# A decay attention and two MLPs on one core: the second products' first two blocks side by side, and another order of the work

## The chip, the core and the metric

The kernel runs on one core of a Trainium2 chip. Five engines work side by side, each through its own instructions in order: TensorE (PE: matrix products into PSUM), VectorE (DVE), ScalarE (ACT), GpSimd (POOL) and SyncE (SP, which here only issues DMAs). The metric is the device time of one execution in microseconds; three runs of the kernel before gave 709.08 to 711.84, median 710.28.

## The reference

Three parts follow each other. The attention has batch 2, 8 heads, 768 positions, head size 64; per block of positions it is `(q k^T * decay) v + (q * decay) state`, and the state takes in `k^T v`. Its output, as 1536 tokens of 512 numbers, goes through two MLPs without residual:

```
h = x @ w_in            # 1536x512 @ 512x2048
x = (h * cos(h)) @ w_out        # first MLP (layer 0); the second has h * sigmoid(h) (layer 1)
```

All is float32.

## The kernel before

**Accuracy.** Matrix products of the MLPs run on a reduced float format. Each operand is split in a high part (a cast on ACT) and a low part (original minus high, on POOL), and a product takes three matmuls: high by high, low by high, high by low. `split` (L122) does it for weights (`win`, `wout`), activations (`gh`, `gl`) and inputs (`xah`/`xal`, `xbh`/`xbl`). Weights are loaded as `raw` (three staging buffers), and made float by an ACT pass (L106) and two DVE passes (L117, L118).

**Attention** (L701 to L738): six chunks of 128 positions. TensorE transposes k and q, makes scores `psc`, multiplies with the state and with v into `pso`; DVE scales the scores (`at`, L326) and keeps the state (L308); `att_x` (L351) takes `pso` out as the first MLP's input with differences `xt`.

**First products** (`gemm_in`, L481): a scheme with seven products instead of eight for a 2x2 division of the operands. A "quad" is a pair of 128-wide slices of the hidden layer, j = 0 to 7, for part A (1024 tokens, 512 columns a matmul) or part B (512 tokens, 256 columns). Each of its seven products takes six matmuls into the PSUM banks a, b (one tile `cab`) and d. Between them ACT copies bank a to b (`copy_ab`, L412) and b to `u2`, `u4` (L416), DVE adds them to d (L421, L424), and the function is applied: in layer 0 `act_n` (L433), `act_s` (L442, DVE), `act_sin` (L449) and `act_g` (L455, DVE), which writes `gd` to DRAM. Products of the next quad are issued between those of the current one.

**Second products** (`gemm_outs`, L652): three blocks of 512 tokens one after the other, four PSUM banks `y` each. Per hidden slice f (16) `prepare` loads `gf` for two slices (L534), splits one (ACT L124, POOL L127), and twelve matmuls follow (L573). During block 0 the weights f = 4 to 15 are converted as well. `keep_a0`, `keep_a1`, `keep_b` turn layer 0's `y` into layer 1's input; `send` writes layer 1's.

Nothing reorders the work: each engine's instructions stand in the order in which the code calls them (a manual schedule), with tasks hung on loop steps by tables in the main loop. Tiles come from pools with a given number of buffers, and an instruction waits until its buffer is free. All large loads and stores go through SP's queue in order: an issue that waits for a buffer holds up those behind it.

Of the kernel before, what the change touches and what calls it, by code (L numbers as in the profile page):

```python
# [16 lines left out]
P = 128  # L17
# [22 lines left out]
def tile_decay_attention__two_mlps(  # L40
# [70 lines left out]
    def convert_w(*piece):  # L111
        if piece not in w32:
            rebias_w(*piece)
# [8 lines left out]
    def split(engine, hi, lo, of):  # L122
        if engine is nc.scalar:
            nc.scalar.copy(hi, of)  # L124
        else:
            engine.tensor_copy(hi, of)
        nc.gpsimd.tensor_tensor(out=lo, in0=of, in1=hi.bitcast(F32), op=ALU.subtract)  # L127
# [14 lines left out]
    def split_plain(L, j):  # L142
        t = wring[j // 2 % 2].tile([P, 2, UNITS, 2 * P], F32R, name="win")
        win[L, j] = t
        w0, w1 = w32.pop((L, 2 * j, 0)), w32.pop((L, 2 * j + 1, 0))
        split(nc.scalar, t[:, 0, 0:2].rearrange("p u c -> p (u c)"), t[:, 1, 0:2].rearrange("p u c -> p (u c)"), w0)
        split(nc.scalar, t[:, 0, 2], t[:, 1, 2], w1[:, 2 * P:])

    def split_sums(L, j):
        t = win[L, j]  # L150
        s = sums.pop((L, j))
        for i in range(2):
            u = slice(3 + 2 * i, 5 + 2 * i)
            split(nc.scalar, t[:, 0, u], t[:, 1, u], s[:, 2 * i:2 * i + 2])

    def split_out(L, f):
        t = wring[0 if f < 7 else 1].tile([P, 2, TB], F32R, name="wout")
        split(nc.scalar, t[:, 0], t[:, 1], w32.pop((L, f, 1)))
        wout[L, f] = t

    def pair_tasks(L, j):
        f = 2 * j
        return [
            lambda: (convert_w(L, f, 0), load_next()),
            lambda: (convert_w(L, f + 1, 0), load_next()),
            lambda: (sum_w(L, j), split_plain(L, j)),
# [3 lines left out]
    def out_tasks(L, f):  # L170
        return [lambda: (convert_w(L, f, 1), load_next()), lambda: split_out(L, f)]
# [48 lines left out]
    qkv, tr, at, kd, sdec, state, pkv, po = {}, {}, {}, {}, {}, {}, {}, {}  # L220
# [130 lines left out]
    def att_x(c):  # L351
        part, n = ("A", c) if c < CA else ("B", c - CA)
        h, l = (x[:, :, :, n * P:(n + 1) * P] for x in x_tiles(0, part))
        ps = po.pop(c).rearrange("p b (u t) i -> p b u t i", t=2)
        b1, b2 = ps[:, 0], ps[:, 1]
        xc = ap_2.tile([P, B, 2, P], F32, tag="xc", name="xc", bufs=1)
        t = ap_2.tile([P, 4, 2, P], F32, tag="xt", name="xt", bufs=1)
        nc.scalar.copy(xc, ps[:, :, 0])
        nc.scalar.copy(h[:, 0:2], b1)
        nc.scalar.copy(h[:, 2], b2[:, 1])  # L360
        nc.vector.tensor_tensor(out=t[:, 0], in0=b2[:, 0], in1=xc[:, 0], op=ALU.subtract)
        nc.vector.tensor_tensor(out=t[:, 1], in0=b2[:, 1], in1=t[:, 0], op=ALU.subtract)
# [95 lines left out]
    def ends(Q):  # L458
        return [
            lambda: (act_sin(Q, 0), act_s(Q, 1)),  # L460
            lambda: act_g(Q, 0),
            lambda: act_sin(Q, 1),
            lambda: act_g(Q, 1),
        ]

    def gemm_in(L, tasks, begun):

        qs = quads[L]
        if not begun:
            product(qs[0], 1)  # L470
            product(qs[0], 7)
            copy_ab(qs[0])
            late = keep_b()
            late.pop(0)()
            product(qs[0], 6)
            late.pop(0)()
            product(qs[0], 2)
            tasks[0] = late + tasks[0]
        copy_u(qs[0], "u2")
        old = []  # L480
        for n, Q in enumerate(qs):  # L481
            more = list(tasks.get(n, []))

            def task():
                if more:
                    more.pop(0)()

            def end():
                if old:
                    old.pop(0)()  # L490

            nxt = qs[n + 1] if n + 1 < len(qs) else None
            if nxt:
                product(nxt, 1)
            end()
            if nxt:
                copy_ab(nxt)
            task()
            product(Q, 5)
            copy_u(Q, "u4")  # L500
            c22(Q)
            end()
            if nxt:
                product(nxt, 7)
                product(nxt, 6)
                copy_u(nxt, "u2")
            else:
                gemm_out(L, 0, 0, (0, 1))
            end()
            task()  # L510
# [3 lines left out]
            end()  # L514
            act_n(Q, 0)
            act_s(Q, 0)
            if not nxt:
                gemm_out(L, 0, 1, (0, 1))
                prepare(L, 0, 2)
# [3 lines left out]
            while more:  # L523
                task()
            old = ends(Q)
        for x in old:
            x()


    gf, gt, ys = {}, {}, {}  # L530

    def load_g(L, b, j):
        t = tpool.tile([P, 2, TB], F32, tag="t4", name="gf", bufs=4)
        nc.sync.dma_start(  # L534
            out=t, in_=gd[L][2 * j:2 * j + 2, :, b * TB:(b + 1) * TB].rearrange("f p c -> p f c")
        )
        gf[L, b, j] = t

    def prepare(L, b, f):
        if f >= FT:  # L540
            b, f = b + 1, f - FT
            if b == NB:
                return
        if (L, b, f // 2) not in gf:
            load_g(L, b, f // 2)
        t = gf[L, b, f // 2][:, f % 2]
        gh, gl = (tpool.tile([P, TB], F32R, tag="t2", name=n, bufs=5) for n in ("gh", "gl"))
        split(nc.scalar, gh, gl, t)
        gt[L, b, f] = gh, gl
# [11 lines left out]
    def gemm_out(L, b, f, ms=range(4)):  # L561
# [15 lines left out]
    def keep_a0():  # L577

        y = ys[0, 0]
        h, l = x_tiles(1, "A")  # L580
        kept["x0"] = yring.tile([P, 4, TB], F32, name="x0")

        def one(u):
            nc.scalar.copy(h[:, u], y[u])
            nc.scalar.copy(kept["x0"][:, 2 * u:2 * u + 2], y[u])
            nc.vector.tensor_tensor(out=l[:, u], in0=y[u], in1=h[:, u].bitcast(F32), op=ALU.subtract)

        return [lambda: one(0), lambda: one(1)]

    def keep_a1():  # L590
        y = ys[0, 1]
        h, l = x_tiles(1, "A")
        x0 = kept["x0"]
        b12 = yring.tile([P, 2, TB], F32, name="b12")
        t = [yring.tile([P, 2, TB], F32, name="T") for _ in range(4)]

        def first():
            nc.scalar.copy(b12, y[0])
            nc.vector.tensor_tensor(out=t[0], in0=y[0], in1=x0[:, 0:2], op=ALU.subtract)

        def second(i):
            nc.scalar.copy(h[:, 2, i], y[4 + i])
            nc.vector.tensor_tensor(out=t[1][:, i], in0=y[4 + i], in1=t[0][:, i], op=ALU.subtract)
            nc.vector.tensor_tensor(out=t[2][:, i], in0=y[4 + i], in1=b12[:, i], op=ALU.subtract)
            nc.vector.tensor_tensor(out=l[:, 2, i], in0=y[4 + i], in1=h[:, 2, i].bitcast(F32), op=ALU.subtract)

        def third(i):
            if i == 3:
                nc.vector.tensor_tensor(out=t[3], in0=x0[:, 2:4], in1=t[1], op=ALU.subtract)
            for m in range(2):  # L610
                split(nc.scalar, h[:, 3 + i, m], l[:, 3 + i, m], t[i][:, m])

        return [first, lambda: second(0), lambda: second(1)] + [lambda i=i: third(i) for i in range(4)]

    def keep_b():
# [7 lines left out]
        def sub(o, x, z):  # L623
            nc.vector.tensor_tensor(out=o, in0=x, in1=z, op=ALU.subtract)

        def first():
            nc.scalar.copy(yc, y[0])
            nc.scalar.copy(h[:, 0], b11)
            sub(t[0], b12, yc[:, :, 0:HB])
            sub(l[:, 0], b11, h[:, 0].bitcast(F32))  # L630

        def second():
            nc.scalar.copy(h[:, 1], b21)
            nc.scalar.copy(h[:, 2], b22)
            sub(t[1], b22, t[0])
# [5 lines left out]
        def third(i):  # L641
            split(nc.scalar, h[:, 3 + i], l[:, 3 + i], t[i])
# [3 lines left out]
    def send(b, m):  # L646
        o = tpool.tile([P, TB], F32, tag="u", name="o", bufs=3)
# [4 lines left out]
    def gemm_outs(L, tasks):  # L652

        for b in range(NB):
            for f in range(FT):
                if L == 1 and b == NB - 1 and f >= FT - 2:
                    break
                prepare(L, b, f + 2) if (b, f) != (0, 0) else None
                if b == 0 and f < 2:
                    gemm_out(L, b, f, (2, 3))  # L660
# [161 lines left out]
```

## Time and profile before

| | us |
|---|---|
| median of three runs | 710.28 (709.08 to 711.84) |
| the profiled execution: its own time, its span | 713.8, 712.0 |
| TensorE busy (matmul) | 601.7 (85%) |
| POOL, ACT, DVE busy | 348.1, 313.1, 286.6 |

TensorE's busy time holds stretches at half clock, so it is not the work at full speed. The stages, by the starts of instructions in the trace: attention to 62.0, hand-over to 91.8, first products of layer 0 to 238.2, second products to 412.5; layer 1 the same to about 552.8 and 708.2; then the last output. In the groups below, a row of the timeline gives the engine's idle time before the instruction in brackets, and what ended it.

### The profile page before, as it was taken

How to read it: one execution, taken by the hardware profiler on the slowest of the kernel's cores; microseconds unless marked ns; L12 is line 12 of the kernel's file. 1: busy time of each engine (PE TensorE's matmuls, PEld its weight loads, DVE VectorE, ACT ScalarE, POOL GpSimd, SP SyncE). 2: the span in 40 equal slices, each digit the busy share in tenths (PEclk: the TensorE clock that was granted, in tenths of full speed). 3: DMA queues.
4: the chain of work that ended last, by engine and by line, in shares of the span. 5: the costliest groups of instructions: out<-in, count | busy, mean ns of one | idle time of the engine just before them, and what ended most of it. 6: DMA issues, size and time to landing. Idle time of an engine off the chain costs nothing.

```text
span 712.0 us, 8935 instructions
## 1 busy us (share of the span) xinstructions
PE 601.7 (85%) x3313; PEld 484.6 (68%) x3313; DVE 286.6 (40%) x397; ACT 313.1 (44%) x518; POOL 348.1 (49%) x299
## 2 busy tenths in 40 slices
PE   8887588888887667889996897999998566999996
PEld 5776366777776545678884676877777444788884
DVE  5674336566664643310044025544455444300101
ACT  4444256677765533342253246555545234322220
POOL 3456435444422266545469816554433366644542
PEclk9998799999999899899999999999999899999999
DMA  9991125344434454643303303654435646352611
GB/s 181 217 226 61 60 59 178 118 149 149 147 133 164 156 177 168 200 130 113 90 5 119 112 1 118 196 176 162 148 137 184 211 174 207 102 166 59 200 38 59
DMA packets 83324, 97.06 MB, mean 136 GB/s; under 512 B 40784, under 2 KB 57168, under 8 KB 83280
## 3 DMA queue, kind: packets, MB, share of 16 engines
q1 hardware_dynamic: 81040, 95.96, 43.1%
q10 hardware_dynamic: 2240, 0.53, 0.4%
q8 instruction: 26, 0.43, 0.3%
q14 instruction: 18, 0.15, 0.1%
HBM read 68.16 MB, written 28.31 MB: 135 GB/s over the span
## 4 chain that ended last, share of the span: by engine, by line
PE 53%; ACT 14%; DMA 11%; DVE 9%; issue 5%; POOL 5%; SPq 2%; POOLq 0%; ACTq 0%; DVEq 0%
PE y L573 25%; PE cab L394 19%; DMA gf<-gd 10%; PE d L394 5%; ACT s L433 3%; ACT u L416 2%; ACT gh L124 2%; ACT w L106 2%; DVE w L118 2%; POOL gl L127 2%; ACT s L449 2%; DVE s L455 2%; PE pso L346 1%; DVE h L424 1%; DVE s L442 1%
## 5 line engine op out<-in xcount | busy, mean ns | idle before, releaser
L127 POOL TENSOR_TENSOR gl<-gf,gh 128x512 fp32r<-128x512 f32 x96 | 131.3, 1368 | 138.4 <-PE y L573 80.9
L124 ACT CAST gh<-gf 128x512 fp32r<-128x512 f32 x96 | 59.4, 619 | 176.7 <-PE y L573 108.9
L573 PE MATMUL y<-gh,wout 128*128 128x512 f32 x384 | 128.2, 417 | 0.0
L573 PE MATMUL y<-wout,gh 128*128 128x512 f32 x384 | 119.6, 393 | 0.0
L394 PE MATMUL cab<-xah,win 128*128 128x512 f32 x320 | 92.9, 413 | 21.0 <-ACT u L416 9.5
L573 PE MATMUL y<-gl,wout 128*128 128x512 f32 x192 | 82.6, 430 | 29.1 <-POOL gl L127 29.1
L118 DVE SCALAR_TENSOR_TENSOR w<-w,sb 128x512 uint32<-128x512 uint32 x64 | 55.2, 862 | 110.9 <-ACT w L106 106.9
L573 PE MATMUL y<-wout,gl 128*128 128x512 f32 x192 | 77.3, 403 | 21.4 <-POOL gl L127 19.5
L573 PEld LDWEIGHTS y<-gh,wout 128*128 128x128 f32 x384 | 78.8, 205 | 17.0
L394 PEld LDWEIGHTS cab<-xah,win 128*128 128x128 f32 x320 | 58.4, 195 | 40.1 <-ACT u L416 15.4
L573 PEld LDWEIGHTS y<-wout,gh 128*128 128x128 f32 x384 | 73.0, 190 | 14.9
L394 PE MATMUL cab<-xbh,win 128*128 128x256 f32 x320 | 56.1, 299 | 19.7 <-ACT u L416 13.5
L573 PEld LDWEIGHTS y<-gl,wout 128*128 128x128 f32 x192 | 39.1, 204 | 44.2 <-POOL gl L127 36.4
L127 POOL TENSOR_TENSOR wout<-w,wout 128x512 fp32r<-128x512 f32 x32 | 44.7, 1396 | 49.9 <-ACT wout L124 49.9
L394 PEld LDWEIGHTS cab<-xbh,win 128*128 128x128 f32 x320 | 46.8, 193 | 28.3 <-ACT u L416 17.6
L573 PEld LDWEIGHTS y<-wout,gl 128*128 128x128 f32 x192 | 36.5, 190 | 34.8 <-POOL gl L127 25.3
L139 POOL TENSOR_TENSOR S<-w 128x256 f32<-128x256 f32 x32 | 27.8, 869 | 60.9 <-DVE w L118 60.9
L394 PE MATMUL cab<-xal,win 128*128 128x512 f32 x160 | 51.0, 400 | 0.0
L127 POOL TENSOR_TENSOR win<-S,win 128x512 fp32r<-128x512 f32 x32 | 44.1, 1400 | 11.9 <-ACT win L124 11.9
L127 POOL TENSOR_TENSOR win<-w,win 128x512 fp32r<-128x512 f32 (+1 forms) x32 | 33.1, 1058 | 25.0 <-ACT win L124 25.0
L648 DVE COPY o<-y 128x512 f32<-128x512 f32 x12 | 8.0, 689 | 92.3 <-PE y L573 89.8
L117 DVE TENSOR_SCALAR sb<-raw 128x512 uint32<-128x512 uint32 x64 | 43.3, 676 | 0.9
(116 smaller groups left out, 895.7 us busy)
## 6 DMA issues: line engine op xcount, KB each, us to landing
gf<-gd SPq DMA_DIRECT2D x48, 512.0 KB, 4.5
raw<-in_moe_w_in_dram SPq DMA_DIRECT2D x32, 512.0 KB, 4.1
gd<-s SPq DMA_DIRECT2D x32, 512.0 KB, 2.8
raw<-in_moe_w_out_dram SPq DMA_DIRECT2D x32, 512.0 KB, 3.3
gd<-s SPq DMA_DIRECT2D x32, 256.0 KB, 2.6
v<-in_v_dram SPq DMA_DIRECT2D x12, 256.0 KB, 5.8
out_dram<-o SPq DMA_DIRECT2D x12, 256.0 KB, 2.5
k<-in_k_dram SPq DMA_DIRECT2D x6, 256.0 KB, 5.9
```

The source lines that it names most:

```text
L106: nc.scalar.activation(w, raw[piece][:, :, 1].bitcast(F32), AF.Prelu, scale=2.0**-112, alpha=-(2.0**32))
L117: nc.vector.tensor_scalar(out=sb, in0=r[:, :, 0], scalar1=2.0**-29, scalar2=7.0, op0=ALU.mult, op1=ALU.min)
L118: nc.vector.scalar_tensor_tensor(out=w, in0=w, scalar=3, in1=sb, op0=ALU.logical_shift_left, op1=ALU.bitwise_or)
L124: nc.scalar.copy(hi, of)
L127: nc.gpsimd.tensor_tensor(out=lo, in0=of, in1=hi.bitcast(F32), op=ALU.subtract)
L139: nc.gpsimd.tensor_tensor(out=s[:, i], in0=x, in1=y, op=op)
L394: nc.tensor.matmul(Q.banks[bank], w[:, part, wu, kt * P:(kt + 1) * P], x[:, xu, kt, :], start=start and m == 0 and kt == 0, stop=m == 2 an ...
L416: nc.scalar.copy(t, Q.banks["b"])
L433: nc.scalar.activation(t, source(Q, i), AF.Identity, scale=1.0 / (2.0 * math.pi), bias=quarter)
L449: nc.scalar.activation(t, t, AF.Sin, scale=2.0 * math.pi, bias=half_pi)
L455: nc.vector.tensor_tensor(out=t, in0=source(Q, i), in1=t, op=ALU.mult)
L573: nc.tensor.matmul(y[m], x, z, start=f == 0 and n == 0, stop=f == FT - 1 and n == 2)
```

## The change

- **Second products.** Blocks 0 and 1 run together: a step of block 0 for slice f, then one of block 1 for slice f-2, with eight banks. One load (`load_g`) now holds one slice for both blocks, `prepare` splits 1024 columns at once into seven slots that lie where `xah`/`xal` lay, and loads are issued four slices ahead, splits two ahead. In a group of three matmuls the one with the low activation comes last.
- **Weights.** A weight's three stages (ACT pass, DVE passes with the next load, split) are separate tasks in consecutive places; seven output weights are converted in the first products, nine in the second.
- **First products.** `copy_ab` and `act_sin` of the previous quad stand earlier, `act_s` stands behind `c21`, the last four quads are 6A, 7A, 6B, 7B.
- **Attention.** `att_x` only copies; the differences (`att_t`) and low parts (`att_l`) follow in the next chunk, behind the state and the first scores; some low parts go from DVE to POOL.
- **Layer 0's output.** Part A is kept by one copy (`copy_a`) and treated during block 2, half of its low parts on DVE.

```diff
     def pair_tasks(L, j):
...
+            lambda: rebias_w(L, f, 0),
+            lambda: (rebias_w(L, f + 1, 0), convert_w(L, f, 0), load_next()),
+            lambda: (convert_w(L, f + 1, 0), load_next(), sum_w(L, j)),
+            lambda: split_plain(L, j),
             lambda: split_sums(L, j),
...
+    def att_l(c):
+        h, l, ps, xc, t = xs.pop(c)
         nc.scalar.copy(h[:, 3:7], t)
+        engine = nc.gpsimd if c < CA - 1 else nc.vector
...
             if nxt:
                 product(nxt, 1)
-            end()
-            if nxt:
                 copy_ab(nxt)
-            task()
+            if old:
+                act_sin(old, 0)
             product(Q, 5)
             copy_u(Q, "u4")
+            if old:
+                act_g(old, 0)
             c22(Q)
-            end()
+            task(2 * n)
+            if old:
+                act_sin(old, 1)
             if nxt:
                 product(nxt, 7)
                 product(nxt, 6)
...
             product(Q, 4)
             c21(Q)
             act_n(Q, 1)
...
+            act_s(Q, 0)
+            act_s(Q, 1)
...
     def gemm_outs(L, tasks):
...
+        items = [x for f in range(FT + 2) for x in ((0, f), (1, f - 2)) if 0 <= x[1] < FT]
+        items += [(2, f) for f in range(FT)]
+        for b, f in items:
...
+            if b == 0:
+                load_g(L, 0, f + 4)
+                prepare(L, 0, f + 2)
...
+            gemm_out(L, b, f, (2, 3) if b == 0 and f < 2 else range(4))
...
     # the main loop's tables, two lines
-                tasks[at_n] = p[0:2]
+                place(tasks, min(4 * j - 8, 18), pair_tasks(L, j))
```

SP's queue from the start of layer 0's second products, before (`gf` is the activations' load, `raw` a weight's, `gd` a write of activations):

```order
L92 DMA raw<-in_moe_w_out_dram 128x1024
L456 DMA gd_74<-s 128x1024 x2
L534 DMA gf<-gd_74 128x2x512
L456 DMA gd_74<-s 128x512 x2
L92 DMA raw<-in_moe_w_out_dram 128x1024 x2
L534 DMA gf<-gd_74 128x2x512
L92 DMA raw<-in_moe_w_out_dram 128x1024 x2
L534 DMA gf<-gd_74 128x2x512
```

And now:

```order
L545 DMA gf<-gd_74 128x1024 x2
L472 DMA gd_74<-s 128x1024
L92 DMA raw<-in_moe_w_out_dram 128x1024
L472 DMA gd_74<-s 128x512
L545 DMA gf<-gd_74 128x1024 x2
L472 DMA gd_74<-s 128x512 x3
L545 DMA gf<-gd_74 128x1024 x4
L92 DMA raw<-in_moe_w_out_dram 128x1024
L545 DMA gf<-gd_74 128x1024
L92 DMA raw<-in_moe_w_out_dram 128x1024
```

Eight loads of activations stand ahead of the first weight of the second products, and then they alternate one by one; before, each stood behind two weights.

ScalarE in one pair of layer 0's first products, before (`s` from `cab` or `h` is `act_n`, `s` from `s` is `act_sin`, `cab` is `copy_ab`):

```order
L433 ACTIVATE s<-h_1340,consts 128x1024
L449 ACTIVATE s<-s,consts 128x1024
L412 COPY cab<-cab 128x512
L124 CAST win<-w 128x512
L124 CAST win<-w 128x256
L416 COPY u_1419<-cab 128x256
L416 COPY u_1437<-cab 128x512
L449 ACTIVATE s<-s,consts 128x1024
L124 CAST win<-S 128x512 x2
```

And now:

```order
L449 ACTIVATE s<-h_1325,consts 128x1024
L428 COPY cab<-cab 128x512
L465 ACTIVATE s<-s,consts 128x1024
L432 COPY u_1398<-cab 128x256
L465 ACTIVATE s<-s,consts 128x1024
L432 COPY u_1429<-cab 128x512
L121 CAST win<-w 128x512
L121 CAST win<-w 128x256
```

`copy_ab` has moved ahead of the first `act_sin`, both of these stand ahead of `u2` (the second `u`), and the weight's casts behind it.

GpSimd from the attention into the first products, before (`S` and `win` are of the weights, `xbl` is the low part of a chunk):

```order
L368 TENSOR_TENSOR xbl<-xt,xbh 128x8x128
L127 TENSOR_TENSOR win<-S,win 128x512 x2
L368 TENSOR_TENSOR xbl<-xt,xbh 128x8x128
L139 TENSOR_TENSOR S<-w 128x256
L139 TENSOR_TENSOR S<-S,w 128x256
L139 TENSOR_TENSOR S<-w 128x256
L139 TENSOR_TENSOR S<-w,S 128x256
L127 TENSOR_TENSOR win<-w,win 128x512
```

And now:

```order
L122 TENSOR_TENSOR win<-S,win 128x512 x2
L382 TENSOR_TENSOR xbl<-xt,xbh 128x8x128
L134 TENSOR_TENSOR S<-w 128x256
L134 TENSOR_TENSOR S<-S,w 128x256
L134 TENSOR_TENSOR S<-w 128x256
L134 TENSOR_TENSOR S<-w,S 128x256
L122 TENSOR_TENSOR win<-w,win 128x512
L122 TENSOR_TENSOR win<-w,win 128x256
L122 TENSOR_TENSOR win<-S,win 128x512 x2
L382 TENSOR_TENSOR xbl<-xt,xbh 128x8x128
```

The second weight pair's operations have moved ahead of the last chunk's low part.

## Rows read from the trace of the kernel before

**Rows 1.** windows: length, each engine's busy us (instructions), clock, DMA share, GB/s
```profile
131.96:185.27 53.31, 47.03 (x252) 38.59 (x253) 34.23 (x49) 37.48 (x61) 24.77 (x24) 1.00 0.44 148
185.27:238.21 52.94, 43.25 (x216) 35.50 (x217) 32.66 (x43) 32.17 (x49) 17.73 (x14) 0.94 0.42 148
238.21:304.95 66.74, 46.22 (x158) 33.84 (x156) 25.05 (x29) 25.51 (x43) 35.15 (x26) 0.87 0.56 186
369.44:412.53 43.09, 34.47 (x132) 26.46 (x132) 11.97 (x8) 13.83 (x25) 38.11 (x33) 0.92 0.30 98
509.05:552.75 43.70, 39.49 (x217) 33.44 (x218) 21.51 (x32) 22.16 (x38) 15.58 (x14) 1.00 0.46 162
552.75:603.58 50.83, 31.67 (x120) 22.78 (x119) 22.29 (x25) 19.01 (x33) 27.00 (x20) 0.93 0.57 194
603.58:708.20 104.62, 102.43 (x444) 82.86 (x444) 11.25 (x15) 24.23 (x40) 51.45 (x39) 1.00 0.34 110
```

**Rows 2.** timeline of one turn in layer 0's block 0: start, us, engine, line
```profile
264.12 0.62 ACT L124 CAST gh<-gf 128x512 fp32r<-128x512 f32 x1 [3.28 <-DMA gf<-gd]
268.82 0.43 SPq L534 DMA_DIRECT2D gf<-gd  x1
273.20 0.62 ACT L124 CAST gh<-gf 128x512 fp32r<-128x512 f32 x1 [3.29 <-DMA gf<-gd]
```

**Rows 3.** windows of twelve matmuls each, behind a wait of TensorE
```profile
284.97:289.41 4.44, 4.44 (x12) 3.46 (x13) 2.99 (x4) 2.34 (x4) 3.21 (x3) 0.62 0.51 148
289.41:292.13 2.72, 2.72 (x13) 2.07 (x12) 0.05 (x1) 0.00 (x0) 1.20 (x1) 1.00 0.91 337
```

**Rows 4.** timeline of one pair of first products in layer 0
```profile
153.27 1.23 DVE L442 SCALAR_TENSOR_TENSOR s<-cab,s 128x1024 f32<-128x1024 f32 x1 [0.70 <-ACT s L433]
154.64 0.66 PE L394 MATMUL cab<-xbh,win 128*128 128x256 f32 x4
155.12 1.15 ACT L433 ACTIVATE s<-h,consts 128x1024 int32<-128x1024 f32 x1 [1.89 <-DVE h L424]
155.37 1.07 PE L394 MATMUL d<-xah,win 128*128 128x512 f32 x4
157.85 1.20 PE L394 MATMUL cab<-xah,win 128*128 128x512 f32 x4 [0.96 <-ACT cab L412]
160.19 1.19 PE L394 MATMUL cab<-xah,win 128*128 128x512 f32 x4 [0.68 <-ACT u L416]
167.49 0.74 PE L394 MATMUL cab<-xbh,win 128*128 128x256 f32 x4 [0.46 <-ACT u L416]
```

**Rows 5.** timeline of one chunk of the attention
```profile
52.10 1.09 PE L242 MATMUL pt<-ident,k 128*128 128x128 f32 x8
54.08 0.68 DVE L308 TENSOR_TENSOR state<-pkv,sdec 128x512 f32<-128x512 f32 x1
55.42 1.16 PE L324 MATMUL psc<-qT,kT 64*128 64x128 f32 x14 [1.80 <-DVE at L326]
```

**Rows 6.** the tile k: from its DMA issues to landing
```profile
DMA to landing us min/median/max: 3.3/5.2/7.0
```

**Rows 7.** timeline of SyncE's queue, the last load of k
```profile
42.27 3.06 SPq L237 DMA_DIRECT2D k<-in_k_dram  x2
```

**Rows 8.** timeline from the attention into the first products
```profile
81.26 2.36 POOL L368 TENSOR_TENSOR xbl<-xt,xbh 128x1024 fp32r<-128x1024 f32 x1 [10.09 <-ACT xbh L367]
83.58 0.72 POOL L139 TENSOR_TENSOR S<-w 128x256 f32<-128x256 f32 x1
87.74 1.22 PE L394 MATMUL cab<-xah,win 128*128 128x512 f32 x2 [4.76 <-POOL win L127]
```

**Rows 9.** timeline in layer 0's third block, GpSimd and VectorE
```profile
373.21 2.31 DVE L609 TENSOR_TENSOR T<-x,T 128x1024 f32<-128x1024 f32 x1
376.60 2.72 POOL L127 TENSOR_TENSOR xal<-T,xah 128x512 fp32r<-128x512 f32 x2
```

**Rows 10.** timeline at the start of layer 1
```profile
436.40 1.22 PE L394 MATMUL cab<-xbh,win 128*128 128x256 f32 x4 [2.45 <-ACT u L416]
```

More of the change, by code (lines that the diff above doesn't have):

```diff
@@ L120, in convert_w, with split @@
         )
[L122 to L127, printed above, removed]
+    def split(hi, lo, of, engine=None):
+        nc.scalar.copy(hi, of)
+        (engine or nc.gpsimd).tensor_tensor(out=lo, in0=of, in1=hi.bitcast(F32), op=ALU.subtract)
     sums = {}
@@ L505, in gemm_in @@
                 product(nxt, 6)
-                copy_u(nxt, "u2")
             else:
                 gemm_out(L, 0, 0, (0, 1))
-            end()
-            task()
+            if old:
+                act_g(old, 1)
+            if nxt:
+                copy_u(nxt, "u2")
+            task(2 * n + 1)
             if nxt:
@@ L522, in gemm_in, with load_g @@
             act_n(Q, 1)
[L523 to L532, printed above, removed]
-        t = tpool.tile([P, 2, TB], F32, tag="t4", name="gf", bufs=4)
[L534 to L537, printed above, removed]
-    def prepare(L, b, f):
[L540 to L549, printed above, removed]
+            act_s(Q, 0)
+            act_s(Q, 1)
+        for i in range(2):
+            act_sin(Q, i)
+            act_g(Q, i)
+    gf, gt, ys, slab = {}, {}, {}, {}
+    SLOTS = 7
+    def load_g(L, b, f):
+        if f >= FT or (L, b, f) in gf or (L, b, f) in gt:
+            return
+        t = tpool.tile([P, 2, TB], F32, tag="t4", name="gf", bufs=4)
+        if b == 0:
+            nc.sync.dma_start(out=t.rearrange("p b c -> p (b c)"), in_=gd[L][f, :, 0:2 * TB])
+            gf[L, 0, f] = t
+        else:
+            nc.sync.dma_start(out=t, in_=gd[L][f:f + 2, :, 2 * TB:].rearrange("f p c -> p f c"))
+            for i in range(2):
+                gf[L, 2, f + i] = t[:, i]
+    def prepare(L, b, f):
+        if f >= FT or (L, b, f) in gt:
+            return
+        t = gf.pop((L, b, f))
+        if b == 0:
+            if L not in slab:
+                slab[L] = [xpool.tile([P, SLOTS, 2, TB], F32R, tag=n, name=m) for n, m in (("xah", "gh"), ("xal", "gl"))]
+            gh, gl = (x[:, f % SLOTS] for x in slab[L])
+            split(gh, gl, t)
+            for i in range(2):
+                gt[L, i, f] = gh[:, i], gl[:, i]
+        else:
+            gh = tpool.tile([P, TB], F32R, tag="t2", name="gh", bufs=5)
+            gl = tpool.tile([P, TB], F32R, tag="u", name="gl", bufs=3)
+            split(gh, gl, t)
+            gt[L, b, f] = gh, gl
     def y_tiles(L, b):
@@ L575, in tile_decay_attention__two_mlps @@
     kept = {}
-    def keep_a0():
-        y = ys[0, 0]
-        h, l = x_tiles(1, "A")
[L581 to L595, printed above, removed]
-        def first():
[L598 to L613, printed above, removed]
@@ new lines, in sub, with copy_a, keep_a, second @@
+    def sub(o, x, z, engine=None):
+        (engine or nc.vector).tensor_tensor(out=o, in0=x, in1=z, op=ALU.subtract)
+    def copy_a(u):
+        if u == 0:
+            kept["x"] = yring.tile([P, 2, 2, TB], F32, name="x")
+        nc.scalar.copy(kept["x"][:, u], ys[0, 0][u])
+    def keep_a():
+        y = ys[0, 1]
+        x = kept["x"]
+        b11, b21, b12, b22 = x[:, 0], x[:, 1], y[0], y[4:6]
+        xc = yring.tile([P, 2, TB], F32, name="b12")
+        t = [yring.tile([P, 2, TB], F32, name="T") for _ in range(4)]
+        h, l = x_tiles(1, "A")
+        def first():
+            nc.scalar.copy(xc, b12)
+            sub(t[0], b12, b11)
+            for i in range(2):
+                sub(t[1][:, i], b22[i], t[0][:, i])
+        def second():
+            for i in range(2):
+                nc.scalar.copy(h[:, 2, i], b22[i])
+                sub(t[2][:, i], b22[i], xc[:, i])
+            sub(t[3], b21, t[1])
+        def third():
+            for i in range(2):
+                sub(l[:, 2, i], b22[i], h[:, 2, i].bitcast(F32))
+        def plain(u):
+            split(h[:, u], l[:, u], x[:, u], nc.vector)
+        def rest(i):
+            split(h[:, 3 + i], l[:, 3 + i], t[i], nc.vector if i % 2 else nc.gpsimd)
+        return [first, second, third] + [lambda f=f, i=i: f(i) for f, i in ((plain, 0), (rest, 2), (plain, 1), (rest, 0), (rest, 1), (rest, 3))]
@@ L763, in tile_decay_attention__two_mlps, with place @@
         tpool = ctx.enter_context(tc.tile_pool(name="tpool", bufs=1, reuse_waits="tile"))
+        copy_u(first, "u2")
+        def place(tasks, at_n, fns):
+            for i, x in enumerate(fns):
+                tasks.setdefault(at_n + i, []).append(x)
         for L in range(2):
@@ new lines, in tile_decay_attention__two_mlps @@
+                tasks.setdefault((1, FT - 1), []).append(lambda: kept.setdefault("a", keep_a()).pop(0)())
+                for i in range(8):
+                    tasks.setdefault((2, i), []).append(lambda: kept["a"].pop(0)())
+                for j, ns in enumerate(((3, 4, 5, 7, 8), (8, 9, 10, 11, 12))):
+                    for n, x in zip(ns, pair_tasks(1, j)):
+                        tasks.setdefault((2, n), []).append(x)
+            else:
+                for m in range(4):
+                    tasks.setdefault((1, FT - 3 + m // 2), []).append(lambda m=m: send(0, m))
+                    tasks.setdefault((2, m), []).append(lambda m=m: send(1, m))
```

200 lines of the change are left out of this document (99 added, 101 removed).

## The prediction

> **What bounds the kernel now.** I read the windows by stage first, because TensorE's 85% is a mean over stages with different limits. In block 0 of layer 0's second products TensorE is busy 46.2 of 66.7 us at a mean clock of 0.87; in the end of block 2 POOL is busy 38.1 of 43.1 us. Layer 1 has the first dip too, 31.7 of 50.8 us, and then 102.4 of 104.6 us full [rows 1]. So what stalls the second products is block 0, not matmul work.
>
> The timeline of one turn there shows a loop. ACT's cast of `gf` starts at 264.12, having waited for the load; the weight passes stand behind it; SP's two `raw` issues wait for buffers that those passes free; the next `gf` is issued behind them at 268.82 and is cast at 273.20 [rows 2]. A turn is 273.20 - 264.12 = 9.08 us and feeds 24 matmuls. At full clock twelve take 2.72 us, and right behind such a wait twelve took 4.44 at a mean granted clock of 0.62, part of them at the lower of the two levels (1.2 and 2.4 GHz): a slow restart costs 1.7 us [rows 3]. So 5.44 us of work stand in a turn of 9.08.
>
> Outside of that, the first products of layer 0 repeat every 53.31 / 3 = 17.77 us per pair of quads [rows 1], with TensorE waiting for ACT's copies [rows 4]; the attention's scores wait for VectorE [rows 5]; and in the hand-over between the two TensorE waits for POOL [rows 8].
>
> **The change part by part.** All sums go against the profiled execution (span 712.0, own time 713.8), which lies 0.5% above the median of the runs, 710.28.
>
> *Second products, layer 0.* I take the stretch from 185.27, where the regular pairs end, to 412.53, the first product of layer 1: 227.3 us [rows 1]. Its work is unchanged. At 185.27 the last two products of quad 5A are to come, four of 5B, and seven each of 6A, 7A, 6B, 7B: 16 large ones at 1.36 us (six matmuls, half of the twelve in rows 3) and 18 small ones at 0.73 (154.64 to 155.37 in rows 4), 21.8 + 13.1 = 34.9. 576 `y` matmuls at 2.72 per twelve are 130.6. Together 165.5 us.
> Waits that I expect to stay: (a) `u2` copies in the last quads, 0.7 + 0.7 + 2.0 + 2.6 = 6.0: the first two like the wait at 160.19, the last two because `act_n`, two `act_sin` (1.15 each for part A, rows 4) and a weight's pass stand ahead of a copy while TensorE's small products take only 0.73; (b) the start: the first `gf` is issued on SP behind a weight's `raw` that waits for VectorE; with 4.4 us from issue to cast (268.82 to 273.20 in rows 2), a 1024-wide cast and a POOL pass of 2.4 to 2.7 [rows 8, 9] TensorE waits 3.0 us for `gh` and 2.0 for `gl`, and 2.0 once more for the second slice: 7.0; (c) four slow restarts of 1.7: 7 [rows 3]; (d) block 2, where POOL holds 14 `gl` (1.36 each, half of the pair in rows 9), two 1024-wide `xal` (2.72) and for two weight pairs 2 x (4 x 0.72 + 3.5 x 1.36) = 15.3 [rows 8, 9], 39.8 us in all. It can't use the first 8 us fully, since `gl` has three buffers, so it ends about 44 us into the block where TensorE would want the last `gl` at 15 x 2.72 = 40.8; VectorE's new low parts beside it stretch POOL's passes further, and I take 6 of the 0 to 12 that the ends give (bounded by POOL as busy as in the 43.1 us of rows 1, and by passes stretched as VectorE's 2.31 is); (e) 1 for the rest. 165.5 + 6 + 7 + 7 + 6 + 1 = 192.5, against 227.3: **-35** (bounds -57, with no wait left, and 0).
> Why the loop goes: per slice now one load, one 1024-wide split and at most one weight, under 24 matmuls = 5.44 us. POOL needs 2.4 to 2.7 + 1.36 = 4.1, ACT about 2.4. The chain load, cast, weight pass, `raw`, next load still exists, but the load behind it is four slices ahead: 9.08 / 4 = 2.3 us a slice. What is late next is therefore TensorE itself, if the transfers keep up: 1.05 MB per 5.44 us is 193 GB/s, and 186 and 194 were moved in the two block-0 stretches [rows 1].
> Against (d) stands this. A row shows a 1024-wide VectorE subtraction with both inputs in SBUF at 2.31 us while POOL's two passes took 2.72 [rows 9]. The Trainium skill (SBUF — State Buffer, "Who interferes with whom") says that a VectorE tensor_tensor with two SBUF inputs and a GpSimd operation that reads SBUF exclude each other for a whole instruction. By it each of the five such 1024-wide subtractions that block 2 now has would add its full time to POOL's, and (d) would be an estimated 9 and not 6. The sum would be 3 higher.
>
> *Second products, layer 1.* From 509.05 to 708.20, 199.2 us [rows 1]. The work is the same 165.5. Here the function has no sine passes, so ACT comes to the copies earlier: (a) 2.4; (b) 2.9 + 2.5 + 1.9 = 7.3; (c) two restarts, 3.5; (d) none, POOL has only `gl`; (e) 1. Sum 179.7: **-20** (bounds -33 and 0).
>
> *First products, layer 0.* In rows 4, with t from 153.27, where a quad's last product has ended: VectorE does `act_s` first (1.23 us), so ACT's `act_n` of the other source starts only at 155.12 (t = 1.85); `copy_ab` stands behind it and behind `act_sin`, and TensorE waits until 157.85 (4.6), and for `u2` until 160.19 (6.9). Now the addition comes first (half as wide, 0.7), `act_n` ends at 1.9, `copy_ab` at 2.4 and is no longer waited for: one small and three large products fill TensorE until 4.8. ACT has `act_sin` twice in the meantime and `u2` is out at 5.5: 1.4 earlier. In the pair's second half it turns: `act_n` and `copy_ab` (to t = 9.7), `act_sin` (10.4), `u4` (11.0), two casts and a weight pass (12.6) and the other `act_sin` (13.2) stand ahead of `u2`, which is out at 13.5, where it was at 167.49 - 153.27 = 14.2: only 0.7 of the 1.4 to 1.5 is left. 17.8 becomes 17.0. Three pairs before 185.27 give 2.3, the first four quads, with the same waits, about 2. **-4** (bounds -8 and +3).
>
> *Attention.* The state and scores no longer stand behind the differences: the state starts at 54.08 although its products were done when k's transposes began at 52.10, and the second scores wait until 55.42 [rows 5]. By the engines alone a chunk would go from 10.4 to some 8 us, five times. But the loads don't allow it: SP's issues are nearly gapless, the last two parts of k are issued from 42.27 to 45.33 and take 5.2 to land [rows 6, 7], so k is there at about 50, 2 us before its use at 52.10. What is left is 2 there and 3.7 in the last chunk's own tail: **-5** (bounds -6 and +1).
>
> *Hand-over.* TensorE waits for POOL's weight low part until 87.74; POOL did the last chunk's `xbl` first (81.26) and then the weight's `S` (83.58) [rows 8]. Now the weight's passes stand ahead. Counted in the new order from the last regular chunk's end (62.0 before): the first pair's `S`, now converted a chunk later, ends 3.3 after it and its first low part 1.4 later; products, scores and inter products in turn end with the last intra products at about 12.6; ACT's copies and casts of the second pair follow to 15.3, POOL's low parts (3.5 x 1.36 = 4.8 us) to 19.4. The second pair's product that ran at 91.76, 29.7 after the chunk's end, then runs at 19.4: **-10** (bounds -13 and 0, where the late first `S` holds up all that follows).
>
> *Start of layer 1.* `u2` there was late until 436.40 [rows 10], behind weight casts; the casts now come after it and part B's splits earlier: **-4** (bounds -5 and +1). The regular pairs of layer 1 I leave as they are: `copy_ab` is earlier, but two casts stand ahead of one `u2`.
>
> Sum: -35 - 20 - 4 - 5 - 10 - 4 = **-78**; 713.8 - 78 = 635.8, and by the median of the runs 710.3 - 78 = **632**.
>
> **The rivals.**
> *Transfers set the pace* of the double block. For it: the stretches before block 0 moved 148 GB/s [rows 1]. Against: 186 and 194 behind it. At 150 a slice with a weight takes 1.05 MB / 150 = 7.0 us, 1.6 over, for eleven slices in two layers 34: 666.
> *Attention and hand-over give nothing*, since loads and POOL bound them: only the second products remain, 710.3 - 55 = 655.
> *Fewer waits than I count*: start-up and POOL hidden better, -20: 612.
> *The loop stays, one load in flight* (the slower side): if a load were still held until the weight ahead of it is converted, each of the 16 slices would cost a turn of 9.08 over both blocks where the forecast has 5.44: 3.64 x 16 x 2 = 116, so 632 + 116 = 748. It decides from 7.9 us a slice on, where the 78 are gone (78 / 32 = 2.4 over 5.44). Against it: eight loads stand ahead of the first weight.
>
> **How the numbers follow.** Forecast 0.55, transfers 0.13, nothing in front 0.16, fewer waits 0.12, loop 0.04. The likeliest is 632, its own range 618 to 650. The range takes in 612 and 666: 612 to 668. A measurement of this kernel can tell about 0.5% from no change. Faster by more: all but the loop, 0.95; within: 0.01; slower 0.04.
>
> **What would show it.** Right: the double blocks as a stretch with TensorE at the full clock and twelve matmuls in 2.72 us; `gf` landing long before its cast; one dip at each start and one at the end of layer 0's block 2 with POOL as releaser; about 57 us to the end of the attention and 17 a pair. Wrong: `gl` or `gf` as releaser all through the double blocks; DMA shares near 1 there; k's loads landing after 51 us; layer 0's block 2 longer than 56 us.

## The result and the profile after

The changed kernel takes 654.6 us (four runs, 650.3 to 656.8) beside 709.9 for the kernel before: a ratio of 0.921, interval 0.916 to 0.926. The forecast was 632. 654.6 lies in the stated range of 612 to 668, but outside the forecast's own 618 to 650. The profiled execution's own time is 654.5, 59.3 less than the 713.8 of before. By stages, each cut at the same matmul of the two traces:

| stage (start before / after) | before | after | change | forecast |
|---|---|---|---|---|
| attention, to the last chunk's scores | 62.0 | 57.7 | -4.3 | -5 |
| hand-over (62.02 / 57.71) | 29.7 | 21.9 | -7.9 | -10 |
| first quads of layer 0 (91.76 / 79.59) | 40.2 | 41.7 | +1.5 | -2 |
| three regular pairs (131.96 / 121.25) | 53.3 | 59.3 | **+6.0** | -2 |
| layer 0's second products (185.27 / 180.53) | 227.3 | 192.4 | **-34.9** | -35 |
| layer 1's first products (412.53 / 372.89) | 96.5 | 96.3 | -0.2 | -4 |
| layer 1's second products (509.05 / 469.21) | 199.2 | 179.6 | **-19.6** | -20 |

So the second products came out at the forecast size, and some 15 of the missing 19 us lie in the first products. The windows of the changed kernel, in the columns of [rows 1]:

```profile
121.25:180.53 59.28, 48.97 (x253) 41.14 (x253) 40.48 (x51) 38.54 (x63) 26.22 (x25) 0.93 0.42 142
180.53:238.99 58.46, 47.99 (x217) 39.87 (x218) 41.21 (x47) 35.42 (x53) 24.36 (x18) 0.83 0.53 182
238.99:328.27 89.28, 89.28 (x396) 73.91 (x395) 45.91 (x29) 33.76 (x48) 55.17 (x27) 1.00 0.48 161
328.27:372.89 44.62, 40.78 (x172) 32.93 (x171) 22.07 (x16) 18.63 (x30) 39.12 (x30) 0.96 0.26 83
417.72:469.21 51.49, 45.78 (x253) 38.74 (x253) 31.30 (x39) 27.40 (x51) 25.85 (x24) 1.00 0.48 164
469.21:648.80 179.59, 171.28 (x780) 140.62 (x780) 76.67 (x69) 60.56 (x92) 97.12 (x58) 0.98 0.44 155
518.70:642.48 123.78, 123.75 (x546) 102.15 (x545) 43.82 (x29) 33.82 (x48) 69.38 (x39) 1.00 0.38 132
```

The double block runs from 238.99 with TensorE busy all the time at a granted clock of 1.00, where block 0 of before had 46.2 of 66.7 us [rows 1]. The regular pairs have the clock at 0.93, where it was 1.00, and take longer. A pair's second half shows why (timeline; in brackets the idle time ahead and its releaser):

```profile
153.26 0.73 ACT L449 ACTIVATE s<-h,consts 128x512 int32<-128x512 f32 x1 [0.49 <-DVE h L440]
154.95 0.59 ACT L432 COPY u<-cab 128x512 f32<-128x512 f32 x1
155.43 1.14 ACT L121 CAST win<-S 128x512 fp32r<-128x512 f32 x2
156.47 0.66 ACT L106 ACTIVATE w<-raw 128x512 f32<-128x512 f32 x1
157.03 0.71 ACT L465 ACTIVATE s<-s,consts 128x512 f32<-128x512 f32 x1
157.64 0.35 ACT L432 COPY u<-cab 128x256 f32<-128x256 f32 x1
158.05 0.74 PE L410 MATMUL cab<-xbh,win 128*128 128x256 f32 x4 [1.76 <-ACT u L432]
158.87 1.70 PE L410 MATMUL cab<-xah,win 128*128 128x512 f32 x4
```

Two casts and a weight's pass, 1.14 + 0.66, stand ahead of the sine and the copy `u2`, and TensorE waits 1.76 in one piece; the waits of before were 0.96, 0.68 and 0.46 apart [rows 4]. Behind this wait four matmuls take 1.70 us, against 1.07 at full clock. In the pair that follows ACT itself stands still, since all four `w` tiles are held until GpSimd's low part has read one:

```profile
173.99 1.98 POOL L122 TENSOR_TENSOR win<-w,win 128x512 fp32r<-128x512 f32 x2
175.31 0.67 ACT L106 ACTIVATE w<-raw 128x512 f32<-128x512 f32 x1 [4.71 <-POOL win L122]
175.88 0.67 ACT L449 ACTIVATE s<-cab,consts 128x512 int32<-128x512 f32 x1
180.53 1.22 PE L410 MATMUL cab<-xbh,win 128*128 128x256 f32 x4 [2.06 <-ACT u L432]
```

### The profile page after: what moved, and what is told of

Its sections match the earlier page's. It is cut to its first block, busy times and chain, and to the rows that moved or that the text cites. A ratio compares the mean times of both kernels' runs of the same rounds, so it can differ in the third digit from the quotient of the medians.

```text
span 652.6 us, 8744 instructions
## 1 busy us (share of the span) xinstructions
PE 586.1 (90%) x3313; PEld 482.2 (74%) x3313; DVE 360.8 (55%) x387; ACT 307.8 (47%) x482; POOL 356.1 (55%) x267
## 4 chain that ended last, share of the span: by engine, by line
PE 67%; ACT 11%; POOL 6%; DVE 5%; DMA 5%; issue 3%; SPq 1%; ACTq 0%; POOLq 0%; DVEq 0%
PE y L591 37%; PE cab L410 21%; PE d L410 8%; ACT u L432 3%; ACT s L465 2%; DMA v<-in_v_dram 2%; POOL win L122 2%; POOL S L134 2%; ACT win L121 2%; ACT s L449 2%; POOL gl L122 1%; DMA gf<-gd 1%; DVE w L116 1%; DMA q<-in_q_dram 1%; DVE sb L115 1%
## 5 line engine op out<-in xcount | busy, mean ns | idle before, releaser
L122 POOL TENSOR_TENSOR gl<-gf,gh 128x1024 fp32r<-128x1024 f32 (+1 forms) x64 | 122.4, 1918 | 98.6 <-ACT gh L121 73.9
L591 PE MATMUL y<-gh,wout 128*128 128x512 f32 x384 | 120.5, 396 | 2.2 <-ACT gh L121 2.2
L410 PE MATMUL cab<-xah,win 128*128 128x512 f32 x320 | 93.8, 416 | 14.3 <-ACT u L432 11.7
L116 DVE SCALAR_TENSOR_TENSOR w<-w,sb 128x512 uint32<-128x512 uint32 x64 | 90.3, 1411 | 20.0 <-ACT w L106 14.0
L121 ACT CAST gh<-gf 128x1024 fp32r<-128x1024 f32 (+1 forms) x64 | 52.9, 831 | 98.6 <-PE y L591 35.8
L591 PEld LDWEIGHTS y<-wout,gh 128*128 128x128 f32 x384 | 72.5, 190 | 19.6 <-ACT gh L121 2.6
L134 POOL TENSOR_TENSOR S<-w 128x256 f32<-128x256 f32 x32 | 33.8, 1056 | 87.8 <-DVE w L116 87.8
L591 PE MATMUL y<-gl,wout 128*128 128x512 f32 x192 | 76.7, 399 | 5.5 <-POOL gl L122 5.5
L122 POOL TENSOR_TENSOR wout<-w,wout 128x512 fp32r<-128x512 f32 x32 | 50.8, 1589 | 42.0 <-ACT wout L121 42.0
L115 DVE TENSOR_SCALAR sb<-raw 128x512 uint32<-128x512 uint32 x64 | 67.8, 1059 | 0.7
L440 DVE TENSOR_TENSOR h<-d,u 128x512 f32<-128x512 f32 (+1 forms) x32 | 17.8, 556 | 64.7 <-PE d L410 64.7
L410 PE MATMUL cab<-xal,win 128*128 128x512 f32 x160 | 51.5, 404 | 0.0
L106 ACT ACTIVATE w<-raw 128x512 f32<-128x512 f32 x64 | 42.8, 669 | 7.8 <-POOL win L122 7.8
```

Of the source, the lines that this page charges most:

```text
L106: nc.scalar.activation(w, raw[piece][:, :, 1].bitcast(F32), AF.Prelu, scale=2.0**-112, alpha=-(2.0**32))
L116: nc.vector.scalar_tensor_tensor(out=w, in0=w, scalar=3, in1=sb, op0=ALU.logical_shift_left, op1=ALU.bitwise_or)
L122: (engine or nc.gpsimd).tensor_tensor(out=lo, in0=of, in1=hi.bitcast(F32), op=ALU.subtract)
L134: nc.gpsimd.tensor_tensor(out=s[:, i], in0=x, in1=y, op=op)
L410: nc.tensor.matmul(Q.banks[bank], w[:, part, wu, kt * P:(kt + 1) * P], x[:, xu, kt, :], start=start and m == 0 and kt == 0, stop=m == 2 an ...
L440: nc.vector.tensor_tensor(out=Q.h2[:, 0], in0=Q.banks["d"], in1=Q.u2, op=ALU.add)
```

## Experiments

Each edit is on the changed kernel unless told otherwise; times are medians. The kernel before took 711.8, 711.6 and 714.6 beside the three groups of runs (experiments 1 to 4, 5 to 8, 9 and 10) and 709.9 beside the changed kernel, so some 3 us between runs of different groups tell nothing; ratios are to the kernel before in the same group.

**1. Weight tasks behind `u2`.**
```diff
             c22(Q)
-            task(2 * n)
...
                 copy_u(nxt, "u2")
+            task(2 * n)
             task(2 * n + 1)
```


> Both weight tasks of a quad now stand behind ACT's copy u2. Theory (casts and rebias, 1.14 + 0.66 us, stand ahead of u2 in ACT's order and are the 1.77 us that TensorE waits in the second half of a pair): that wait falls to some 0.5; the regular pair of layer 0 goes from 17.6 to 16.3, of layer 1 from 17.0 to 16.3; with fewer slow restarts 654.6 becomes about 640. Rival (the wait is the chain of act_n, VectorE and act_sin, whatever the casts): 653 to 656. Rival (weights then come too late): 660 or more, with win as releaser of TensorE.


Measured 647.8 (ratio 0.908, 0.902 to 0.915).

```profile
149.47 0.73 ACT L465 ACTIVATE s<-s,consts 128x512 f32<-128x512 f32 x1
150.37 0.37 ACT L432 COPY u<-cab 128x256 f32<-128x256 f32 x1 [0.17 <-PE cab L410]
150.64 1.14 ACT L121 CAST win<-S 128x512 fp32r<-128x512 f32 x2
150.80 0.74 PE L410 MATMUL cab<-xbh,win 128*128 128x256 f32 x4 [0.46 <-ACT u L432]
```

`u2` now waits for TensorE and not the other way; pairs take 16.3 in both layers, as the theory said, with no lower clock between them. The total is 7 better and not 14: the stall of the `w` tiles stayed (a wait of 2.97 at 168.9), and the first `gh` of layer 1's second products, a task like the others, came late (5.05 against 2.35).

**2. Output weights later.**
```diff
-                place(tasks, n - 1, out_tasks(L, f))
+                place(tasks, n if f < 2 else n - 1, out_tasks(L, f))
```


> The tasks of the first two output weights come half a quad later. Theory (ACT stands 4.7 us before a rebias because all four w tiles are held by the two weight pairs that overlap there, and act_n behind it is late): that wait goes, the stretch 158 to 180.5 falls from 22.5 to about 19, layer 1's like stretch by 1: 654.6 becomes about 650. Rival (a later split of the output weights is then missed at the start of the second products): 654 or more.


Measured 650.6 (0.913, 0.908 to 0.919): the third of the three pairs takes 18.1 (159.14 to 177.24) in place of 22.5 (158.05 to 180.53). The theory holds.

**3. Idle pieces filled with zeros.**
```diff
             if nxt:
+                for _ in range(2 if nxt.part == "A" else 6):
+                    nc.tensor.matmul(nxt.banks["d"], zeros[:, 0:P], zeros[:, 0:nxt.n], start=False, ...)
                 product(nxt, 2)
```


> Ahead of every product 2 of a quad, where TensorE waits for u2, it multiplies zeros into a bank of that quad: two such matmuls ahead of an A quad, six ahead of a B quad; the result is unchanged. Theory (the stretches at the lower clock in the first products, each some 1.7 us, come from the idle pieces of 1.8 us and more ahead of them): the granted clock of 121 to 180 goes from 0.93 to near 1.00, five or six restarts are saved, 654.6 becomes about 646. Rival (the lower clock has another cause): the clock stays at 0.93 and the time at 655 to 658.


Measured 648.9 (0.910, 0.904 to 0.915).

```profile
119.22:172.29 53.07, 47.28 (x261) 39.34 (x264) 37.68 (x48) 35.52 (x57) 24.83 (x23) 1.00 0.46 154
```

The pairs keep their 17.6 (119.22, 136.83, 154.46), so no wait of the computation got shorter, and the granted clock of the stretch is 1.00 in place of 0.93. The idle pieces brought the lower clock.

**4. Eight banks without the lead.**
```diff
-                load_g(L, 0, f + 4)
+                load_g(L, 0, f + 2)
```
(and the third and fourth early load left out)


> The double block's gf loads are issued two slices ahead, at the cast's own place in the order, and not four. Theory of the forecast (the loop of load, cast, weight pass, raw, next load is broken by the load that is four slices ahead, not by the eight banks): nine slices a layer with a weight fall back to a turn of about 9.1 us for 5.44: some +30 a layer, 654.6 becomes about 715. Rival (24 matmuls under one load are enough to hide it, whatever the distance): 655 to 660.


Measured 673.2 (two runs), between both, and neither is right. TensorE waits at the start of the double block for `gh`, 6.24 in layer 0, and for `gl` behind it, 1.22, and then not again until block 2. SP's and TensorE's rows:

```profile
243.91 1.22 PE L591 MATMUL y<-gh,wout 128*128 128x512 f32 x2 [6.24 <-ACT gh L121]
257.12 0.33 SPq L92 DMA_DIRECT2D raw<-in_moe_w_out_dram  x1
257.55 0.38 SPq L545 DMA_DIRECT2D gf<-gd  x1
261.35 0.33 SPq L92 DMA_DIRECT2D raw<-in_moe_w_out_dram  x1
261.78 0.38 SPq L545 DMA_DIRECT2D gf<-gd  x1
```

The loop is there, since most casts still wait for their load, but a turn with one weight takes 4.2 to 5.4 us here (the distances of the `raw` issues from 251.76 on), where one with two took 9.08 [rows 2], and it stands under 5.44 of matmuls.

**5. Attention's differences not delayed.** `att_t` and `att_l` are called right behind `att_x` of their chunk.


> The attention's differences and low parts stand right behind their chunk's copies again, not one chunk later. Theory of the forecast (the delay takes VectorE out of the way of state and scores, and the loads then set the pace): the chunks go back to some 10 us from the 8.5 of the changed kernel, the last regular chunk's intra products from 55.0 to about 59.5, and 654.6 becomes 659. Rival (the loads set the pace anyhow): 55 to 56 there, and 654 to 656.


Measured 654.7 (two runs): no difference. The last regular chunk's intra products, here and then in the changed kernel:

```profile
54.67 1.97 PE L346 MATMUL pso<-at,v 128*64 128x128 f32 x32
```
```profile
52.58 0.66 PE L242 MATMUL pt<-ident,q 128*128 128x128 f32 x4 [1.52 <-DMA q<-in_q_dram]
55.01 2.77 PE L346 MATMUL pso<-at,v 128*64 128x128 f32 x32
```

The rival holds. With the delay the chunks take 8.2 and 9.3 at first, and then wait for `q` and `v`; without it they take 9.2 and wait less. Before it was 10.4 and 59.78: what is left of the edit, merged subtractions and two low parts moved from VectorE to GpSimd, is enough for the same time; which of these does it, no run shows.

**6. All low parts of block 2 on GpSimd.**
```diff
-            split(h[:, u], l[:, u], x[:, u], nc.vector)
+            split(h[:, u], l[:, u], x[:, u])
...
-            split(h[:, 3 + i], l[:, 3 + i], t[i], nc.vector if i % 2 else nc.gpsimd)
+            split(h[:, 3 + i], l[:, 3 + i], t[i])
```


> In block 2 of layer 0 all six low parts of the next layer's activations are GpSimd's; four of them were VectorE's. Theory (GpSimd's own passes set the pace there): four more 1024-wide passes of 2.7 us, so up to 11 us, of which its idle time there takes some: 654.6 becomes 661 to 665. Rival (a VectorE subtraction holds GpSimd up for its whole 2.3 us, so that it is no cheaper to give it to VectorE): +2 at most, 655 to 657. The rival is what the Trainium skill (SBUF - State Buffer, Who interferes with whom) makes of such a pair.


Measured 660.0 (two runs), 5.4 more by the medians, and 5.1 more between the same two matmuls of the traces (the first `y` product to layer 1's first product, 142.6 in the changed kernel and 147.7 here): below the theory's 6.5 to 10, above the rival's 2, nearer to the theory. TensorE's waits for `gl` go from 3.23 and 0.61 to

```profile
349.11 0.50 PE L591 MATMUL y<-gl,wout 128*128 128x512 f32 x1 [3.43 <-POOL gl L122]
359.27 0.50 PE L591 MATMUL y<-gl,wout 128*128 128x512 f32 x1 [2.80 <-POOL gl L122]
375.28 0.50 PE L591 MATMUL y<-gl,wout 128*128 128x512 f32 x1 [0.47 <-POOL gl L122]
```

**7. The kernel before, with the lead alone.**
```diff
             load_g(L, b, f // 2)
+        if b == 0 and f % 2 == 0 and 2 <= f < FT - 2:
+            load_g(L, b, f // 2 + 1)
```


> The kernel before, and in block 0 of the second products the load of two slices is issued one pair earlier; nothing else. Theory (the lead of the load is what the loop lacked): TensorE runs near full in block 0, some 17 us less a layer: 711 becomes about 677. Rival (two weights in 24 matmuls are the loop: the passes of VectorE, ACT and GpSimd on two weights and the raw loads behind them; the eight banks have one weight in 24): a turn of 7 to 9 us stays, and 711 becomes 695 to 710.


Measured 681.0 (two runs), 30.7 less than before, close to the theory. ACT's casts:

```profile
255.76 0.61 ACT L124 CAST gh<-gf 128x512 fp32r<-128x512 f32 x1
258.38 0.62 ACT L124 CAST wout<-w 128x512 fp32r<-128x512 f32 x1 [1.42 <-DVE w L118]
258.90 0.61 ACT L124 CAST gh<-gf 128x512 fp32r<-128x512 f32 x1
262.05 0.61 ACT L124 CAST gh<-gf 128x512 fp32r<-128x512 f32 x1
```

No cast waits for a load any more. A slice takes 3.14, a turn of two 6.29 and not 9.08, and its releaser is VectorE's pass on the weight.

**8. The three repairs together.** Weight tasks behind `u2` as in 1, output weights as in 2; `load_g` and `prepare` of the first slices hang on a table of their own, which runs where all tasks ran before.


> Weight tasks behind u2 as in the first experiment, the first two output weights later as in the second, and the first gf casts of the second products left where the changed kernel has them, ahead of u2's copy. Theory (the three waits are separate): pairs of 16.3, no wait of 3 us at 169, and a wait of some 2.3 us in place of 5.05 at the start of layer 1's second products: 639 to 642. Rival (with u2 ahead, the later output weights gain nothing more, or come late): 645 to 648.


Measured **632.9** (0.888, 0.884 to 0.892), better than both kernels and than the theory.

```profile
120.99:169.91 48.92, 45.51 (x252) 38.69 (x252) 38.20 (x51) 39.16 (x63) 25.94 (x23) 1.00 0.50 171
```

Three pairs take 48.9 where the changed kernel had 59.3. The rest stands at the starts: from there to layer 1's first product 187.6 (192.4), and from that to the first `gl` of layer 1 134.7 (139.3).

**9. The old loop of the activations.** In `gemm_in` `act_s(old, 1)` stands ahead of `copy_ab` and the additions, `act_sin(old, 1)` behind `u2`, as before the change.


> The first products' loop puts the activations where the kernel before has them (VectorE's act_s ahead of the next quad's addition, the copy cab behind the first sine); weights, loads and everything else as in the changed kernel. Theory of the forecast (the new order is worth some 0.8 a pair): regular pairs of layer 0 go from 17.6 to 18.4 or more, and 654.6 becomes 658 to 662. Rival (the new order is what made the first products slower than forecast): pairs of 17.8 with waits under 1 us and the clock at 1.00, and 654.6 becomes 648 to 652.


Measured 649.5 (0.910, 0.905 to 0.914), and each side is half right. Regular pairs take 18.7, so the new order does shorten a pair, by 1.1; but its waits are 0.96, 0.68 and 1.4 and the clock of the three stays at 1.00, and the first `gl` of the second products comes 4.5 earlier (228.04 against 232.57).

**10. Experiment 8 with zeros in three places.**


> The kernel of the eighth run with six zero matmuls ahead of product 2 of three quads of layer 0, where its trace still has idle pieces of 2 us and more with the lower clock behind them (103 us, 200 to 210 us). Theory (idle pieces bring the lower clock, 1.2 to 1.7 us a time): two or three restarts saved, 632.9 becomes 629. Rival (these restarts come from other waits beside them): 632 to 634.


Measured 632.6 (ratio 0.885, 0.882 to 0.888, beside 0.888, 0.884 to 0.892 for 8): no difference that these runs can tell, and they don't decide between 629 and 632. The traces say more. The stretch from the end of the three pairs to the first `gh` of the second products, in 8 and then here:

```profile
169.91:215.29 45.38, 37.89 (x192) 31.86 (x192) 36.93 (x42) 30.82 (x48) 21.21 (x17) 0.92 0.52 174
167.78:213.86 46.08, 36.85 (x204) 30.61 (x204) 36.85 (x42) 30.81 (x48) 21.24 (x17) 0.99 0.52 177
```

The granted clock rose where the zeros stand, as the theory said, but the stretch got no shorter: at its end TensorE waits 3.56 for `gh`, where it waited 0.55. Around the first of the three places 27.15 became 26.05 us, so most of what the zeros gained was lost in that wait.

## Why the prediction was right or wrong

**Second products: size right, reason incomplete.** -34.9 and -19.6 stand against -35 and -20. The forecast put the end of the loop down to the load that is four slices ahead ("9.08 / 4 = 2.3 us a slice"). Four kernels tell lead and banks apart:

| | load late | load early |
|---|---|---|
| four banks | 711 | 681 (experiment 7) |
| eight banks | 673 (experiment 4) | 655 |

The two eight-bank kernels hold the other edits too, so only differences along a row are the lead's alone (with eight banks, the early third and fourth load included). It is worth 30 with four banks, where it shortens the turn to 6.29. With eight it is worth 18, and all of that at the start of each layer's second products; in the steady part, one weight in 24 matmuls already makes the turn shorter than the work. The rival of the kept loop, which decided from 7.9 us a slice on, fell by a margin that I had not seen: even with a late load a turn is 4.2 to 5.4. Transfers never set the pace: 161 GB/s were enough in the double block, where TensorE was busy for all of its 89.28 us.

The match of the sums is in part luck. In layer 0 TensorE idles 10.5 us up to the double block and 3.8 in the end of block 2, 14.3 where (a), (b), (d) and (e) made 20; what is left of 192.4 over these and the 165.5 of work is 12.6 of slow stretches, where (c) had 7. In layer 1 it idles 8.3 for 10.7, and 5.8 are left for 3.5. Waits were put too high and slow restarts too low by about as much. That the time came out at the 655 of the rival "attention and hand-over give nothing" is chance too, since the two gave 12.2. (The bound of -57 "with no wait left" should have been -62, 227.3 less 165.5.)

**Block 2 (d).** Forecast 6; TensorE idles 3.2 and 0.6, and with a clock of 0.96 the end of block 2 has 40.8 busy of 44.6. That low parts on VectorE relieve GpSimd was right, but only in part (experiment 6), because the two hold each other up: where two such passes overlap, one ends its own undisturbed time behind the end of the other (rows in the last section). The Trainium skill (SBUF — State Buffer, "Who interferes with whom") calls the port pair that the two share an exclusive lock, and has a VectorE instruction with two SBUF inputs contend with a GpSimd instruction that reads SBUF; this trace agrees.

What was wrong was the price that I put on it. The 2.31 of [rows 9] is a subtraction that had itself been held up, by a GpSimd pass that began before it and ended at 374.44 (the pair of 2.72 that I set beside it began only at 376.60, when it had ended):

```profile
371.44 3.00 POOL L127 TENSOR_TENSOR xal<-T,xah 128x512 fp32r<-128x512 f32 x2
```

In the changed kernel two of VectorE's four low parts take 1.24 and 1.21 us, the other two, held up, 2.21 and 1.76. So experiment 6 takes four times 1.2 of hold-up from GpSimd and gives it four passes of 2.4 to 2.6: an estimate of +5.2 from these rows, against 5.1 between the traces. Theory and rival each had a part of it; the rival's 2, and the 9 for (d) that the prediction worked out by the rule, came from the 2.31.

**First products of layer 0: the step that failed.** "17.8 becomes 17.0" was mis-sized, and two effects had no term. The chain that was counted for `u2` came out: with t from the same matmul (144.02 here) the first copy ends at 5.6 (forecast 5.5), the second at 14.0 (13.5), since `act_n` waited 0.49 for VectorE's addition. That is 17.6 a pair, 1.8 over three. Not counted were slow restarts: I priced them in the second products only, and merging short waits into one of 1.77 brought two into this stretch, some 3.3 (experiment 3). And the stall of 4.7 on the four `w` tiles, from weight tasks that were split finer and overlap, cost some 3 (22.5 less 17.6, less the slow restart in it of 1.7; experiment 2). Together 8.1 of the 8.3 that are missing there. In the first quads `u2` comes 3.28 late at 102.5, which experiment 1 only cut to 2.58; what their +1.5 is made of was not taken apart.

**First products of layer 1.** The start gave 2.8 of the 4. The pairs were left "as they are", although I wrote that two casts stand ahead of one `u2`: they cost 2.6 over three pairs (51.5 against 48.9), and experiment 1 takes that back. I saw this edit and priced it at zero without naming a cover.

**Attention and hand-over.** -4.3 for -5, and the loads are the bound as said, though TensorE waits for `q` (1.52) and `v` and no longer for `k`; but the delay is not what did it (experiment 5). The hand-over gave 7.9 of 10:

```profile
57.71 1.16 PE L324 MATMUL psc<-qT,kT 64*128 64x128 f32 x16
61.82 0.73 PE L410 MATMUL cab<-xah,win 128*128 128x512 f32 x2 [2.17 <-POOL win L122]
64.45 2.07 PE L410 MATMUL cab<-xah,win 128*128 128x512 f32 x4
79.59 0.73 PE L410 MATMUL d<-xah,win 128*128 128x512 f32 x2 [0.31 <-POOL win L122]
```

It takes 21.9 and not 19.4. Behind the first wait TensorE worked at the lower clock (2.07 for four matmuls), the intra products ended at 14.0 and not 12.6, and GpSimd's four low parts took 5.1 and not 4.8.

## What to carry to other kernels

When an order is rewritten, list for each engine what now stands ahead of the copy that the matmul waits for, and give each such edit a price, also where it looks like a detail: 1.8 us of casts in front of one copy cost more than the new loop order had won. Look at the length of the single wait as well as at the sum, since a longer one can be paid a second time in clock. A loop of load, convert, next load is cured by lead or by more work per turn; see which of the two already suffices. And before a duration from a trace becomes a price, look at what the other engines did beside it: it may hold the very wait that the price is meant to add.

## What the runs showed of the hardware

Pairs with waits of 0.96, 0.68 and 0.46 us [rows 4], or with 0.96, 0.68 and 1.4 (experiment 9), ran at a granted clock of 1.00; with waits of 0.68 and 1.77 the clock fell behind two of three such pairs. So the sum does not order them: 3.0 us a pair kept the clock, 2.45 did not always.

VectorE and GpSimd hold each other up for whole passes when both read SBUF alone. VectorE's weight pass `sb` takes 0.42 by itself, a 1024-wide low part 1.24 on VectorE and 2.38 on GpSimd (all of the changed kernel):

```profile
65.22 2.38 POOL L382 TENSOR_TENSOR xbl<-xt,xbh 128x1024 fp32r<-128x1024 f32 x1 [0.29 <-ACT xbh L378]
168.36 0.42 DVE L115 TENSOR_SCALAR sb<-raw 128x512 uint32<-128x512 uint32 x1
329.24 1.27 DVE L596 TENSOR_TENSOR xal<-y,xah 128x512 fp32r<-128x512 f32 x2
329.29 1.30 POOL L122 TENSOR_TENSOR gl<-gf,gh 128x512 fp32r<-128x512 f32 x1 [1.06 <-ACT gh L121]
330.43 1.24 DVE L122 TENSOR_TENSOR xal<-x,xah 128x1024 fp32r<-128x1024 f32 x1
331.66 1.29 POOL L122 TENSOR_TENSOR gl<-gf,gh 128x512 fp32r<-128x512 f32 x1 [1.07 <-PE y L591]
331.82 2.21 DVE L122 TENSOR_TENSOR xal<-x,xah 128x1024 fp32r<-128x1024 f32 x1
332.91 3.39 POOL L122 TENSOR_TENSOR xal<-T,xah 128x1024 fp32r<-128x1024 f32 x1
333.96 2.63 DVE L115 TENSOR_SCALAR sb<-raw 128x512 uint32<-128x512 uint32 x1
```

From 329.24 on they still run side by side: there VectorE reads one input, `y`, from PSUM, and neither is longer for it. From 331.66 on they take turns. GpSimd's `gl` ends at 332.95 and VectorE's second low part at 334.03, 1.1 later; GpSimd's `xal`, begun at 332.91, ends at 336.30, 2.3 behind that; VectorE's `sb`, begun at 333.96, ends at 336.59, 0.3 behind the `xal`. The short pass in second place pays most: over the whole run VectorE's 64 `sb` and 64 `w` passes average 1.06 and 1.41 us, where the shortest take 0.41 and 0.69.
